# Batches 3 to 7 of a fused attention and feed-forward kernel: slots' maxima sent ahead of k and v, slots' work four units later in the plan, attention begun three units ahead

## The chip, the cores and the metric

One core of a Trainium2 chip runs the program. The metric is the device time in microseconds of one execution. The kernel before takes 735.24 us (median of three runs, 733.53 to 735.92).

## The reference, cut to what matters

Eight batches b, eight heads, 576 tokens, head width 64, and 32 memory slots per head. All in float32:

```
a    = softmax(phi, over the 32 slots' own token axis)      # as written: max, exp and sum over the 576 tokens
k_m  = a^T @ k ;  v_m = a^T @ v                             # 32 slots per head
attn = softmax(q @ k_m^T / 8, over the 32 slots)
x    = attn @ v_m, heads side by side                        # [4608, 512]
h    = x @ w_in                                             # [4608, 2048]
g    = where(h > 0, h, exp(min(h, 0)) - 1)
out  = g @ w_out                                            # [4608, 512]
```

phi's maximum over the tokens is one number for each head and slot, 256 numbers a batch, and exp(phi - max) is needed with tokens on the partitions, as the left side of a^T @ k.

## The kernel before, in words

**Attention of one batch.** phi comes twice: as `ph` (128 partitions of slots, 2 x 576 tokens, load_phi, L260) for the maxima and sums, and as three tiles `e` (tokens on the partitions, load_e, L267). phi_max (L407, DVE) takes the negative maxima `nm`, phi_exp (L412, ACT) the sums. spread_max (L272) brings the maxima to all partitions: one DMA writes `nm` (1 KB) to DRAM as `nmd` (L276), a second reads it back to 128 partitions as `nmb` (L278); it waits for the first. e_shift (L289, POOL, three instructions) adds `nmb` to `e`, e_exp (L294, ACT, three) takes the exponentials. slots (L453, PE, 80 small matmuls in one PSUM bank `psb`) makes k_m and v_m; slots_copy (L474, DVE), slots_transpose (L487, PE) and kv_copy (L494, ACT) turn them; scores (L502, PE), and a softmax in DVE and ACT for each of three token groups follow, ending in the tiles `A`. Then v_m is multiplied into w_in, in four pieces: vw (L502, PE) fills both `psb` banks, vw_high (L605, ACT) and vw_low (L611, DVE) split each bank into a high and a low part and give it back. There are two `psb` banks in all, taken in turn by vw, slots, slots_transpose and scores.

**Units.** The feed-forward part is a line of 256 units, 32 a batch, two token halves by 16 groups of 128 channels. Unit n is: hidden (L657, six matmuls into a bank `psh`, two of these), relu of -h (L672) and its exponential (L673) on ACT, elu_max on DVE (L684 for 256 tokens, L686 for the last 32, which also gives the `psh` bank back), elu_high (L698, ACT), elu_low (L704, DVE), project (L712, six matmuls into `pso`). After every second batch the 32 last tokens of the four halves are projected in one go: rest_high (L752), rest_low (L757), rest_project (L712), rest_store (L771 on ACT, then four DMAs, L773). store (L743) writes a half of a batch.

**What sets the order.** A table FIRST gives the order on all engines up to the start of batch 2's units. After it, `at(place, step, ...)` gives each step a place counted in units, and the steps are emitted by place: hidden of unit n at n - 1.7, project at n + 0.6, and attention of batch b from o = 32 b - 22 on. For PE and SP the order by place is the order on the engine. For ACT, DVE and POOL a scheduler chooses: it may put an instruction ahead of others with an earlier place. On each engine the instructions run in the order that results, and a wait holds all that stand behind it. SP runs ahead of the others as far as its waits let it: in each batch it stands at store until the last collect, and then issues the next batch's loads one after the other.

Of the kernel before, what the change touches and what calls it, by code (L numbers as in the profile page):

```python
# [8 lines left out]
F32 = mybir.dt.float32  # L9
# [7 lines left out]
P = 128  # L17
# [10 lines left out]
NB = 2  # L28
# [147 lines left out]
def fused_kernel(ctx: ExitStack, tc: tile.TileContext, phiT, phi, kv0, kvt, kv, q0, q1, w_in, w_out, out):  # L176
# [15 lines left out]
    dram = ctx.enter_context(tc.tile_pool(name="dram", bufs=2, space=bass.MemoryType.DRAM))  # L192
# [6 lines left out]
    def t2k(shape, name):  # L199
        return work.tile(shape, F32, name=name, tag="t2k", bufs=7)  # L200
# [11 lines left out]
    def temp(b, name, i, n):  # L212
# [20 lines left out]
    st = [  # L233
        {"kv": {}, "q": {}, "vw": [None] * NVC, "A": [None, None], "e": {}, "sc": {}, "ps": {}}
        for _ in range(B)
    ]
# [35 lines left out]
    def spread_max(b):  # L272

        s = st[b]
        d = dram.tile([P, 2], F32, name="nmd")
        nc.sync.dma_start(d, s["nm"])  # L276
        s["nmb"] = work.tile([P, P, 2], F32, name="nmb", bufs=1)
        nc.sync.dma_start(  # L278
            s["nmb"].rearrange("p x a -> p (x a)"),
            d.rearrange("x a -> (x a)").partition_broadcast(P),  # L280
        )
# [425 lines left out]
    acc = {}  # L707
# [61 lines left out]
    def rest_store(p):  # L769
        t = t2k([P, DM], "orest")  # L770
        nc.scalar.copy(t, acc.pop(("rest", p)))  # L771
        for n in range(4):
            nc.sync.dma_start(  # L773
                out[2 * p + n // 2, n % 2, NT * P :], t[n * REST : (n + 1) * REST, :]
            )
# [7 lines left out]
    def warm_up(n):  # L783
# [8 lines left out]
        for f in (  # L792
            tables, warm_up, load_phi, load_e, load_kv, load_kv0, load_q, load_half_q, load_raw, dec_mag,
            dec_low, dec_top, dec_add, dec_high, dec_rest, phi_max, phi_exp, slot_scale,
            spread_max, e_shift, e_exp, e_transpose, e_copy, slots, slots_copy, slots_transpose,
            kv_copy, scores, turn, softmax_max, softmax_shift, softmax_exp, softmax_sum,
            softmax_divide, turn_back, probs_high, probs_low, vw, vw_high, vw_low, hidden,
            elu_exp, elu_max, rest_copy, elu_high, elu_low, project, collect, store, rest_high, rest_low,
            rest_project, rest_store,
        )  # L800
    }
# [11 lines left out]
    def at(place, f, *a):  # L813
        if (f, a) not in done:
            plan.append((place, len(plan), f, a))

    def softmax(b, u, o, step):
        at(o, turn, b, u)
        at(o + step, softmax_max, b, u)
        at(o + 1.01 * step, softmax_shift, b, u)  # L820
        at(o + 2 * step, softmax_exp, b, u)
        at(o + 3 * step, softmax_sum, b, u)
        at(o + 3.01 * step, softmax_divide, b, u)
        at(o + 4 * step, turn_back, b, u)
        at(o + 5 * step, probs_high, b, u)
        at(o + 6 * step, probs_low, b, u)

    def products(b, c, o, *cols):
        at(o, vw, b, c, *cols)
        at(o + (0.3 if cols else 0.75), vw_high, b, c, *cols)  # L830
        at(o + (0.31 if cols else 0.76), vw_low, b, c, *cols)

    def attention(b, o):
        at(o - 4, load_phi, b)
        for c in range(NCH):
            at(o - 3 + c, load_kv, b, c)
        for u in range(3):
            at(o + 4 + u, load_q, b, u)
            at(o - 3 + u, load_e, b, u)
            at(o + 1.1 + u, e_shift, b, u)  # L840
            at(o + 2.1 + u, e_exp, b, u)
        at(o + 0.1, phi_max, b)
        for g in range(2):
            at(o + 0.12, phi_exp, b, g)
        at(o + 1.1, slot_scale, b)
        at(o + 1, spread_max, b)
        for c in range(NCH):
            at(o + 5.4, slots, b, c)
        at(o + 6.1, slots_copy, b)
        at(o + 7.2, slots_transpose, b)  # L850
        at(o + 7.4, kv_copy, b)
        for u in range(3):
            i = o + 8.2 + 2 * u
            at(i, scores, b, u)
            softmax(b, u, i + 0.7, 0.3)

    for b in range(2, B):
        base = 2 * NJ * b
        attention(b, 43 if b == 2 else base - 22)
        for c in range(NVC):  # L860
            products(b, c, base - 7.6 + 8 * c)
    for it, (b, hf, j) in enumerate(order):
        at(it - 1.7, hidden, it)
        at(it - 1.69, elu_exp, it)
        at(it - 1.68, elu_max, it)
        if b < NB:
            at(it - 1.67, rest_copy, it)
        at(it - 1, elu_high, it)
        at(it - 0.99, elu_low, it)
        at(it + 0.6, project, it)  # L870
        if ends[it][2]:
            for t in range(NT):
                at(it + 0.7, collect, it, t)
            if j == NJ - 1:
                at(it + 0.8, store, b, hf)
                if b % 2 and hf:
                    for i in range(NJ // 2):
                        at(it + 0.61 + 0.01 * i, rest_high, b // 2, i)
                        at(it + 0.611 + 0.01 * i, rest_low, b // 2, i)
                        at(it + 0.612 + 0.01 * i, rest_project, b // 2, i)  # L880
                    at(it + 0.81, rest_store, b // 2)

    plan.sort(key=lambda x: x[:2])
    with tc.manual_schedule(engines={mybir.EngineType.PE, mybir.EngineType.SP}):
# [48 lines left out]
```

## Time and profile before

| what | value |
|---|---|
| median of three runs | 735.24 us |
| the profiled execution's own time | 735.4 us |
| its span, first to last instruction | 733.6 us |
| mean granted TensorE clock | 0.99 |
| PE busy | 709.2 us, 97% |
| DVE, ACT, POOL busy | 467.2, 465.0, 44.6 us |

A row of the timeline has the start in us, the duration, the engine, the line, the operation with out<-in, the count of instructions that it merges, and in brackets how long the engine stood idle before it and what ended that. SPq is SP's queue of DMA issues. A row of the waits names the engine and line that waited, what it waited for, and then the total in us, the number of times and the longest. A row of the stretches has the two ends in us, then the length, the busy time of each engine, the granted TensorE clock, the DMA share and GB/s.

### The profile page before, as it was taken

What the parts mean: (1) busy time and instruction counts of PE and PEld (TensorE: products, weight loads), DVE (VectorE), ACT (ScalarE), POOL (GpSimd) and SP (SyncE); (2) the same over time, 40 slices, a digit from 0 to 9 for tenths busy, and PEclk for the clock granted to TensorE, in tenths of its full rate; (3) what the DMA queues carried; (4) which work ended last, traced back from release to release, by engine and by line L of the source; (5) the groups of instructions that cost most, each with busy time, mean ns of one, the idle gap of its engine ahead of it and who ended that gap; (6) DMA issues with size and microseconds to landing.
All of it is one profiled execution on the core that took longest, in us unless ns stands there. A gap on an engine that the chain in (4) does not pass through costs nothing.

```text
span 733.6 us, 13668 instructions
## 1 busy us (share of the span) xinstructions
PE 709.2 (97%) x5114; PEld 572.5 (78%) x5114; DVE 467.2 (64%) x1253; ACT 465.0 (63%) x1110; POOL 44.6 (6%) x88
## 2 busy tenths in 40 slices
PE   7688999999999999999999999999999999999997
PEld 6566888888768878877788777887787887888885
DVE  4999899886495467544954449545774447754442
ACT  4768988886456656755655557656565565665552
POOL 0001112123000100010000100000000010000000
PEclk9899999999999999999999999999999999999999
DMA  8960513431316110611015210260002600010002
GB/s 311 370 231 28 203 30 115 149 101 62 101 59 210 28 44 1 239 42 45 2 57 182 56 45 1 75 206 28 18 1 75 218 27 20 1 58 0 2 1 72
DMA packets 24978, 64.46 MB, mean 88 GB/s; under 512 B 3408, under 2 KB 7632, under 8 KB 24912
## 3 DMA queue, kind: packets, MB, share of 16 engines
q1 hardware_dynamic: 24912, 63.59, 25.7%
q8 instruction: 41, 0.67, 0.4%
q14 instruction: 25, 0.20, 0.1%
HBM read 54.13 MB, written 9.44 MB: 87 GB/s over the span
## 4 chain that ended last, share of the span: by engine, by line
PE 68%; DMA 14%; DVE 8%; ACT 5%; issue 2%; POOL 1%; SPq 1%; POOLq 0%; DVEq 0%; ACTq 0%
PE pso L712 41%; PE psh L657 21%; DMA nmd<-nm 6%; PE psb L502 4%; DMA nmb<-nmd 3%; PE psb L453 2%; DMA ph<-phiT 2%; POOL e L289 1%; DMA win<-w_in 1%; ACT gf L673 1%; DMA kvt<-kv 1%; ACT gf L672 1%; DMA e<-phi 1%; DVE gf L681 1%; DVE nm L407 1%
## 5 line engine op out<-in xcount | busy, mean ns | idle before, releaser
L712 PE MATMUL pso<-wout,gp 128*128 128x512 f32 x1728 | 449.6, 398 | 3.3 <-DVE gp L704 2.6
L712 PEld LDWEIGHTS pso<-wout,gp 128*128 128x128 f32 x1728 | 310.1, 188 | 84.2 <-ACT gf L673 13.0
L657 PEld LDWEIGHTS psh<-A,vw 128*128 128x128 f32 x1536 | 229.9, 189 | 39.5 <-issue 6.2
L657 PE MATMUL psh<-A,vw 128*128 128x288 f32 x1536 | 251.1, 299 | 8.6 <-DVE rest L686 3.8
L684 DVE SCALAR_TENSOR_TENSOR gf<-gf,psh 128x256 f32<-128x256 f32 x192 | 80.4, 419 | 130.3 <-ACT gf L673 130.0
L672 ACT ACTIVATE gf<-psh 128x288 f32<-128x288 f32 x256 | 104.7, 409 | 86.3 <-PE psh L657 84.4
L698 ACT CAST gp<-gf 128x256 fp32r<-128x256 f32 x256 | 103.4, 404 | 87.0 <-DVE gf L684 73.4
L704 DVE TENSOR_TENSOR gp<-gf,gp 128x256 fp32r<-128x256 f32 x256 | 107.6, 421 | 55.0 <-ACT gp L698 54.7
L673 ACT ACTIVATE gf<-gf 128x288 f32<-128x288 f32 x256 | 113.7, 444 | 7.8
L611 DVE TENSOR_TENSOR vw<-psb,vw 128x512 fp32r<-128x512 f32 (+2 forms) x74 | 43.3, 602 | 11.7 <-ACT vw L605 11.5
L289 POOL TENSOR_TENSOR e<-e,nmb 128x512 f32<-128x512 f32 (+1 forms) x18 | 19.7, 1122 | 377.1 <-DMA nmb<-nmd 374.8
L681 DVE SCALAR_TENSOR_TENSOR gf<-gf,psh 128x288 f32<-128x288 f32 x64 | 28.9, 452 | 18.2 <-ACT gf L673 16.9
L605 ACT CAST vw<-psb 128x512 fp32r<-128x512 f32 (+2 forms) x74 | 37.1, 522 | 2.9 <-PE psb L502 0.7
L502 PE MATMUL psb<-win,kvm 64*32 64x512 f32 (+2 forms) x592 | 36.0, 541 | 0.0
L694 POOL COPY rest<-gf 128x32 f32<-128x32 f32 x64 | 24.3, 380 | 167.6 <-DVE gf L681 167.5
L686 DVE SCALAR_TENSOR_TENSOR rest<-gf,psh 128x32 f32<-128x32 f32 x192 | 34.2, 179 | 0.1
L752 ACT CAST gp<-rest 128x256 fp32r<-128x256 f32 x32 | 13.0, 406 | 23.8 <-PE pso L712 21.8
L373 DVE SCALAR_TENSOR_TENSOR top<-mag,top 128x512 uint32<-128x512 uint32 x32 | 22.2, 692 | 1.9 <-ACT mag L364 0.3
L757 DVE TENSOR_TENSOR gp<-rest,gp 128x256 fp32r<-128x256 f32 x32 | 13.4, 418 | 15.0 <-ACT gp L752 14.9
L368 ACT ACTIVATE mag<-raw 128x512 uint32<-128x512 uint32 x30 | 20.0, 670 | 2.5 <-DVE top L373 2.5
L294 ACT ACTIVATE e<-e 128x512 f32<-128x512 f32 (+1 forms) x18 | 9.8, 559 | 16.9 <-POOL e L289 16.8
L364 ACT ACTIVATE mag<-raw 128x512 f32<-128x512 f32 x30 | 19.5, 668 | 0.4 <-DVE win L385 0.4
(96 smaller groups left out, 368.4 us busy)
## 6 DMA issues: line engine op xcount, KB each, us to landing
kvt<-kv SPq DMA_DIRECT2D x32, 512.0 KB, 7.4
out<-osb SPq DMA_DIRECT2D x16, 512.0 KB, 2.8
raw<-w_in SPq DMA_DIRECT2D x15, 512.0 KB, 6.0
raw<-w_out SPq DMA_DIRECT2D x15, 512.0 KB, 7.9
qt<-q SPq DMA_DIRECT2D x18, 384.0 KB, 4.3
ph<-phiT SPq DMA_DIRECT2D x7, 576.0 KB, 5.0
e<-phi SPq DMA_DIRECT2D x12, 256.0 KB, 6.3
qh<-q SPq DMA_DIRECT2D x4, 576.0 KB, 11.5
```

Of the source, the lines that this page charges most:

```text
L502: nc.tensor.matmul(outs[a][32 * j : 32 * j + 32, :], lhs[r, 32 * j : 32 * j + 32], rhs[r, j], start=True, stop=True, tile_position=(64 * a ...
L605: nc.scalar.copy(s["vw"][c][:, HI, a, n0:n1], ps)
L611: nc.vector.tensor_tensor(t[:, LO, a, n0:n1], ps, t[:, HI, a, n0:n1], ALU.subtract)
L657: nc.tensor.matmul(ps, t[:, x, g, c0 : c0 + P], s["A"][hf][:, y, g, :], start=(n == 0), stop=(n == 5),)
L672: nc.scalar.activation(gf, ps, AF.Relu, scale=-1.0)
L673: nc.scalar.activation(gf, gf, AF.Exp, scale=-1.0)
L681: nc.vector.scalar_tensor_tensor(gf, gf, -1.0, ps, ALU.add, ALU.max)
L684: nc.vector.scalar_tensor_tensor(gf[:, :n], gf[:, :n], -1.0, ps[:, :n], ALU.add, ALU.max)
L686: nc.vector.scalar_tensor_tensor(rest_of(b, j)[:, o : o + REST], gf[:, n:], -1.0, ps[:, n:], ALU.add, ALU.max)
L698: nc.scalar.copy(gp[:, HI], gs[it][:, : NT * P])
L704: eng.tensor_tensor(gp[:, LO], gf[:, : NT * P], gp[:, HI], ALU.subtract)
L712: nc.tensor.matmul(ps, gp[:, y], wout[j][:, x, :], start=(first and n == 0), stop=(last and n == 2),)
```

## The change: what it does

In attention(b) for b of 3 to 7 (x = 1; batch 2 keeps its places):

- o is 32 b - 25, three units earlier, and with it load_phi and load_e; phi_max, phi_exp and the DMA that writes `nmd` go one more unit ahead.
- spread_max only writes `nmd`; the reading DMA is a step of its own, fetch_max, at o + 1.5. load_kv's five loads begin at o + 1, so that the write of `nmd` stands ahead of all of them, and fetch_max behind the first.
- e_shift, e_exp, slots, slots_copy, slots_transpose, kv_copy and scores get four units (4.4 for the first two) on top of o, so that slots to scores lie one unit later than before in the line of units. load_q lies two units later.
- rest_store keeps the copy on ACT; its four DMAs become rest_out, at the unit's place + 4.6 in place of + 0.81.

```diff
     def spread_max(b):
 
         s = st[b]
-        d = dram.tile([P, 2], F32, name="nmd")
+        d = s["nmd"] = dram.tile([P, 2], F32, name="nmd")
         nc.sync.dma_start(d, s["nm"])
+        if b <= NB:
+            fetch_max(b)
+
+    def fetch_max(b):
+        s = st[b]
+        d = s["nmd"]
         s["nmb"] = work.tile([P, P, 2], F32, name="nmb", bufs=1)
...
     def rest_store(p):
         t = t2k([P, DM], "orest")
         nc.scalar.copy(t, acc.pop(("rest", p)))
+        acc["orest", p] = t
+
+    def rest_out(p):
+        t = acc.pop(("orest", p))
         for n in range(4):
...
     def attention(b, o):
+
+        x = 1 if b > NB else 0
         at(o - 4, load_phi, b)
         for c in range(NCH):
-            at(o - 3 + c, load_kv, b, c)
+            at(o - 3 + 4 * x + c, load_kv, b, c)
         for u in range(3):
-            at(o + 4 + u, load_q, b, u)
+            at(o + 4 + 5 * x + u, load_q, b, u)
             at(o - 3 + u, load_e, b, u)
-            at(o + 1.1 + u, e_shift, b, u)
-            at(o + 2.1 + u, e_exp, b, u)
-        at(o + 0.1, phi_max, b)
+            at(o + 1.1 + 4.4 * x + (1 - 0.3 * x) * u, e_shift, b, u)
+            at(o + 2.1 + 4.4 * x + (1 - 0.3 * x) * u, e_exp, b, u)
+        at(o + 0.1 - x, phi_max, b)
...
-        at(o + 1, spread_max, b)
+        at(o + 1 - x, spread_max, b)
+        if b > NB:
+            at(o + 1.5, fetch_max, b)
         for c in range(NCH):
-            at(o + 5.4, slots, b, c)
-        at(o + 6.1, slots_copy, b)
...
+            at(o + 5.4 + 4 * x, slots, b, c)
+        at(o + 6.1 + 4 * x, slots_copy, b)
...
         for u in range(3):
-            i = o + 8.2 + 2 * u
+            i = o + 8.2 + 4 * x + 2 * u
...
-        attention(b, 43 if b == 2 else base - 22)
+        attention(b, 43 if b == 2 else base - 25)
...
                     at(it + 0.81, rest_store, b // 2)
+                    at(it + 4.6, rest_out, b // 2)
```

The changed file has new lines, so that what is L294 before is L300 in it, and so on: 6 more from L278 on.

**ACT, batch 4's e_exp.** Before, the relu that reads psh_3890 is that of unit 105, and e_exp (L294) stands behind it:

```order
L672 ACTIVATE gf_3897<-psh_3890 128x288
L673 ACTIVATE gf_3897<-gf_3897 128x288
L698 CAST gp_3912<-gf_3897 128x256
L294 ACTIVATE e_3885<-e_3885 128x512
L672 ACTIVATE gf_3922<-psh_3915 128x288
L294 ACTIVATE e_3910<-e_3910 128x512
L673 ACTIVATE gf_3922<-gf_3922 128x288
L605 CAST vw_3950<-psb_3927 128x512
L294 ACTIVATE e_3945<-e_3945 64x256
```

After, the relu that reads psh_3825 is that of unit 102, and e_exp is L300:

```order
L704 CAST gp_3822<-gf_3809 128x256
L678 ACTIVATE gf_3832<-psh_3825 128x288
L679 ACTIVATE gf_3832<-gf_3832 128x288
L300 ACTIVATE e_3820<-e_3820 128x512
L704 CAST gp_3845<-gf_3832 128x256
L300 ACTIVATE e_3843<-e_3843 128x512
L678 ACTIVATE gf_3855<-psh_3848 128x288
L300 ACTIVATE e_3866<-e_3866 64x256
L679 ACTIVATE gf_3855<-gf_3855 128x288
```

The plan's place of e_exp is later than before, but on ACT it stands three units earlier, ahead of the elu_high of unit 102 (L704 that writes gp_3845); in batches 3, 5, 6 and 7 it stands 4, 4.5, 3.5 and 4.5 units earlier.

**PE, batch 4's slots.** Before, slots (L453) follows a hidden, and vw (L502) comes a project and a hidden behind it:

```order
L657 MATMUL psh_4107<-A_3476,vw_3950 128x288 x6
L453 MATMUL psb_4119<-kvt_3883,e_3885 32x128 x8
L453 MATMUL psb_4119<-kvt_3908,e_3885 32x128 x8
L453 MATMUL psb_4119<-kvt_3943,e_3910 32x128 x8
L453 MATMUL psb_4119<-kvt_3973,e_3910 32x128 x8
L453 MATMUL psb_4119<-kvt_4001,e_3945 32x128 x8
L712 MATMUL pso10_3768<-wout7_1317,gp_4080 128x512 x3
L712 MATMUL pso11_3769<-wout7_1317,gp_4080 128x512 x3
L657 MATMUL psh_4173<-A_3405,vw_3950 128x288 x6
L502 MATMUL psb_4185<-win3_80,kvm_3305 32x512 x4
L502 MATMUL psb_4186<-win3_80,kvm_3305 32x512 x4
```

After (vw is L508, slots L459), the two have the same place, and slots stands right behind vw:

```order
L663 MATMUL psh_4126<-A_3426,vw_3960 128x288 x6
L508 MATMUL psb_4138<-win3_80,kvm_3326 32x512 x4
L508 MATMUL psb_4139<-win3_80,kvm_3326 32x512 x4
L459 MATMUL psb_4148<-kvt_3917,e_3820 32x128 x8
L459 MATMUL psb_4148<-kvt_3955,e_3820 32x128 x8
L459 MATMUL psb_4148<-kvt_3983,e_3843 32x128 x8
L459 MATMUL psb_4148<-kvt_4006,e_3843 32x128 x8
L459 MATMUL psb_4148<-kvt_4029,e_3866 32x128 x8
L718 MATMUL pso00_3740<-wout8_1591,gp_4100 128x512 x3
```

With two banks, slots' psb_4148 is the bank that vw's psb_4138 has just filled, and its first matmul waits for DVE. The order is the same in all five batches.

**SP, batch 7's loads**, behind the stores of batch 5 (the loads of batch 5, behind the stores of batch 3, read the same). Before:

```order
L773 DMA out<-orest 32x512 x4
L260 DMA ph<-phiT 128x1152
L300 DMA kvt<-kv 128x1024
L267 DMA e<-phi 128x2x256
L300 DMA kvt<-kv 128x1024
L267 DMA e<-phi 128x2x256
L300 DMA kvt<-kv 128x1024
L267 DMA e<-phi 64x256
L300 DMA kvt<-kv 128x1024
L300 DMA kvt<-kv 64x1024
L276 DMA nmd<-nm 128x2
L278 DMA nmb<-nmd 128x256
```

After:

```order
L260 DMA ph<-phiT 128x1152
L783 DMA out<-orest 32x512 x4
L267 DMA e<-phi 128x2x256 x2
L267 DMA e<-phi 64x256
L276 DMA nmd<-nm 128x2
L306 DMA kvt<-kv 128x1024
L284 DMA nmb<-nmd 128x256
L306 DMA kvt<-kv 128x1024 x3
L306 DMA kvt<-kv 64x1024
L328 DMA qt<-q 128x768 x3
```

The maxima (L276) have moved ahead of all five loads of k and v, phi's load ahead of the rest's stores, and the loads of `e` still stand behind those stores. In batches 4 and 6 there is no rest in front. On DVE, batch 3's phi_max has moved from behind unit 68 into the end of FIRST, between batch 2's turn_back (L567) and its last rest_low instructions (L757); that of batches 5 and 7 into the rest stage; that of batches 4 and 6 stands where it stood.

More of the change, by code (lines that the diff above doesn't have):

```diff
@@ L833, in attention @@
     def attention(b, o):
+        x = 1 if b > NB else 0
         at(o - 4, load_phi, b)
         for c in range(NCH):
-            at(o - 3 + c, load_kv, b, c)
+            at(o - 3 + 4 * x + c, load_kv, b, c)
         for u in range(3):
-            at(o + 4 + u, load_q, b, u)
+            at(o + 4 + 5 * x + u, load_q, b, u)
             at(o - 3 + u, load_e, b, u)
-            at(o + 1.1 + u, e_shift, b, u)
-            at(o + 2.1 + u, e_exp, b, u)
-        at(o + 0.1, phi_max, b)
+            at(o + 1.1 + 4.4 * x + (1 - 0.3 * x) * u, e_shift, b, u)
+            at(o + 2.1 + 4.4 * x + (1 - 0.3 * x) * u, e_exp, b, u)
+        at(o + 0.1 - x, phi_max, b)
         for g in range(2):
-            at(o + 0.12, phi_exp, b, g)
+            at(o + 0.12 - x, phi_exp, b, g)
         at(o + 1.1, slot_scale, b)
-        at(o + 1, spread_max, b)
+        at(o + 1 - x, spread_max, b)
+        if b > NB:
+            at(o + 1.5, fetch_max, b)
         for c in range(NCH):
-            at(o + 5.4, slots, b, c)
-        at(o + 6.1, slots_copy, b)
-        at(o + 7.2, slots_transpose, b)
-        at(o + 7.4, kv_copy, b)
+            at(o + 5.4 + 4 * x, slots, b, c)
+        at(o + 6.1 + 4 * x, slots_copy, b)
+        at(o + 7.2 + 4 * x, slots_transpose, b)
+        at(o + 7.4 + 4 * x, kv_copy, b)
         for u in range(3):
-            i = o + 8.2 + 2 * u
+            i = o + 8.2 + 4 * x + 2 * u
             at(i, scores, b, u)
```

## The prediction

> **What bounds the kernel now.** First the page's busy times, then the waits of PE and ACT from batch 3's loads to the end:
>
> ```profile
> PE 709.2 (97%) x5114; PEld 572.5 (78%) x5114; DVE 467.2 (64%) x1253; ACT 465.0 (63%) x1110; POOL 44.6 (6%) x88
> PE psh L657 <- DVE rest L686: 3.8, 5, 1.1
> PE pso L712 <- DVE gp L704: 0.3, 1, 0.3
> ACT e L294 <- POOL e L289: 14.6, 8, 3.3
> ```
>
> PE bounds the kernel. From batch 3 on it waits 4.1 us in all (3.8 + 0.3), once in each of the five batches. Each time ACT stands at e_exp for POOL's e_shift, and POOL for the maxima. Batch 4's chain, from the timeline:
>
> ```profile
> 305.33 1.35 DVE L407 TENSOR_REDUCE nm<-ph 128x2 f32<-128x1152 f32 x1 [0.52 <-DMA ph<-phiT]
> 307.23 0.33 SPq L276 DMA_DIRECT2D nmd<-nm  x1
> 315.32 0.33 SPq L278 DMA_DIRECT2D nmb<-nmd  x1
> 320.13 3.29 POOL L289 TENSOR_TENSOR e<-e,nmb 128x512 f32<-128x512 f32 x3 [76.53 <-DMA nmb<-nmd]
> 321.48 0.63 ACT L294 ACTIVATE e<-e 128x512 f32<-128x512 f32 x1 [3.19 <-POOL e L289]
> 324.09 0.18 DVE L686 SCALAR_TENSOR_TENSOR rest<-gf,psh 128x32 f32<-128x32 f32 x1
> 324.41 1.04 PE L657 MATMUL psh<-A,vw 128*128 128x288 f32 x6 [0.96 <-DVE rest L686]
> ```
>
> The write of 1 KB takes 8.1 us (307.23 to 315.32), behind k and v in the queue; from the read's issue to e_exp it is another 6.16 us. ACT stands 3.19 us, PE loses 0.96 of it.
>
> **Term 1: e_exp's wait, removed.** If it went altogether: **-4.1 us**.
>
> **Term 2: e_exp's wait, come back longer.** The maxima are now ahead of k and v. The nearest row for a write with nothing in front is batch 2's:
>
> ```profile
> 169.32 0.34 SPq L276 DMA_DIRECT2D nmd<-nm  x1
> 172.48 0.33 SPq L278 DMA_DIRECT2D nmb<-nmd  x1
> ```
>
> 3.16 us. With the 6.16 from above, e_exp's data are there 9.32 us after the write is issued: call that time T. In batch 4 phi_max stands where it stood, so the write goes out at about 307.0, and T = 316.3: 5.2 us sooner than 321.48. But on ACT e_exp stands three units sooner, behind unit 102's exponential:
>
> ```profile
> 310.66 0.44 ACT L673 ACTIVATE gf<-gf 128x288 f32<-128x288 f32 x1
> 314.12 1.55 PE L712 MATMUL pso<-wout,gp 128*128 128x512 f32 x6
> 315.51 0.96 PE L657 MATMUL psh<-A,vw 128*128 128x288 f32 x6
> ```
>
> ACT comes to it at 311.1 and stands 5.2 us. Queued behind it are unit 102's elu_high, which project 102 (314.12) waits for, and unit 103's relu, whose bank hidden 105 (315.51) needs. By the old chain's steps (two e_exp at 0.54, POOL 1.3 apart, relu, exponential, L684, L686) elu_low ends 1.4 us after T and the bank is free 3.6 after T. So project 102 starts at 317.7 (3.6 late), hidden 105 at 319.9: **4.4 us** lost. Batch 6 has the same order, and the same 4.4.
>
> In batches 5, 7 and 3 the loads of `e` stand behind the rest's stores, and the write behind those. Batch 5, and batch 3's rows:
>
> ```profile
> 391.99 1.74 SPq L773 DMA_DIRECT2D out<-orest  x4
> 394.75 0.43 SPq L267 DMA_DIRECT2D e<-phi  x1
> 395.28 0.41 SPq L300 DMA_DIRECT2D kvt<-kv  x1
> 405.53 0.96 PE L657 MATMUL psh<-A,vw 128*128 128x288 f32 x6
> 219.25 1.76 SPq L773 DMA_DIRECT2D out<-orest  x4
> 234.57 0.96 PE L657 MATMUL psh<-A,vw 128*128 128x288 f32 x6
> ```
>
> An issue takes 0.53 us (394.75 to 395.28), so three `e` end at 393.75 + 1.6, the write goes at 395.4, and T = 404.7. Here e_exp stands behind elu_high, as before, and the bank is free 2.93 us after T (324.41 - 321.48): hidden 136 starts at 407.6 instead of 405.53, **2.1**. Batch 7 is laid out alike, 2.1. Batch 3: write at 222.7, T = 232.0, two e_exp ahead of elu_high and the third ahead of the next relu, bank 4.1 after T: 236.1 instead of 234.57, **1.5**. Sum: 4.4 + 4.4 + 2.1 + 2.1 + 1.5 = **+14.5 us**. Bounds: the shortest landing of a store in the profile is 1.7 us, of a load 3.0:
>
> ```profile
> out<-orest SPq DMA_DIRECT2D x16, 64.0 KB, 1.7
> ph<-phiT SPq DMA_DIRECT2D x2, 288.0 KB, 3.0
> kvt<-kv SPq DMA_DIRECT2D x32, 512.0 KB, 7.4
> ```
>
> With these T comes 1.5 + 1.5 us sooner (1.7 for 3.16, and 3.0 for the read's 4.5 or so): 1.4 lost in batches 4 and 6, nothing in the others, +2.8. On the other side the first load of k and v lies between write and read and three 512 KB loads right behind: 1 us more a batch, +19.5. I keep 14.5, since batch 2 is the same transfer.
>
> **Term 3: slots wait for vw's bank, added.** slots now stands on PE right behind vw, and wants the bank that vw_low gives back. Before, slots_transpose wanted the same bank a project later, in batch 4:
>
> ```profile
> 341.32 1.09 PE L502 MATMUL psb<-win,kvm 64*32 64x512 f32 x16
> 342.34 1.65 PE L712 MATMUL pso<-wout,gp 128*128 128x512 f32 x6
> 343.07 0.69 DVE L611 TENSOR_TENSOR vw<-psb,vw 128x512 fp32r<-128x512 f32 x1 [0.21 <-ACT vw L605]
> 343.83 0.42 PE L487 MATMUL psb<-ident,x 128*128 128x128 f32 x2
> ```
>
> The next matmul behind vw starts 1.02 us after it (342.34); the bank is usable 2.51 after it (343.83). The whole line of projects and hiddens stands behind slots. 1.49 us in each of five batches: **+7.5 us**. Lower bound 0.3 a batch, what slots_transpose itself lost there:
>
> ```profile
> PEld psb L487 <- DVE vw L611: 1.3, 5, 0.3
> ```
>
> **Term 4: batch 3's phi_max, moved.** It goes from a DVE that had time into the end of FIRST, where PE waits for DVE's rest_low:
>
> ```profile
> 214.51 0.42 DVE L757 TENSOR_TENSOR gp<-rest,gp 128x256 fp32r<-128x256 f32 x1
> 214.98 1.43 PE L712 MATMUL pso<-wout,gp 128*128 128x512 f32 x5 [0.57 <-DVE gp L757]
> 225.99 1.34 DVE L407 TENSOR_REDUCE nm<-ph 128x2 f32<-128x1152 f32 x1
> ```
>
> PE already waits, so all 1.34 us count: **+1.3** (0 if phi's reduction fits a gap).
>
> **Term 5: the clock.** PE's pauses grow from 1 us to over 3. What pauses do to the granted clock is seen near the start, in stretches of 3.41 us:
>
> ```profile
> 19.77:23.18 3.41, 1.49 (x25) 1.15 (x24) 3.20 (x8) 2.47 (x7) 0.00 (x0) 0.99 1.03 408
> 23.18:26.60 3.42, 3.01 (x44) 2.46 (x46) 3.32 (x8) 2.76 (x6) 0.00 (x0) 0.51 1.03 409
> 36.84:40.25 3.41, 1.89 (x21) 1.37 (x10) 3.31 (x8) 2.50 (x5) 0.00 (x0) 0.99 1.02 408
> 40.25:43.66 3.41, 3.41 (x24) 2.00 (x23) 3.38 (x10) 2.06 (x7) 0.21 (x1) 0.51 1.02 408
> 57.30:60.73 3.43, 2.17 (x22) 1.26 (x21) 3.36 (x11) 3.43 (x9) 0.00 (x0) 1.00 0.00 0
> 60.73:64.10 3.37, 2.32 (x16) 1.86 (x14) 3.30 (x12) 2.01 (x6) 0.34 (x1) 1.00 0.00 0
> ```
>
> A stretch with PE idle for 1.92 (3.41 - 1.49) or 1.52 us is followed by one at 0.51; one with 1.26 idle is not. At 0.51 a stretch loses at most 3.41 x 0.49 = 1.67 us. The pauses of batches 4 to 7 (3.6, 2.1, 3.6, 2.1) are beyond the edge; those of batch 3 and of slots (1.5) lie on it. Four drops at 1.3, since part of a slow stretch is pause: **+5.2** (0 to 12 drops: 0 to 15).
>
> The Trainium skill ("TensorE: Matmul & The Clock Gate", Why this matters for your kernels) asks for no PE gap over some 3 us; by that only batches 4 and 6 would lose clock, and the term would be 2.6. The trace disagrees: 1.52 us was enough.
>
> **At nothing.** k and v land 7.4 us after issue and are needed only at slots, some 20 us later; if late, slots waits. load_q keeps its distance to scores. rest_out changes only SP: the last batch's four stores stay last. phi_max and phi_exp of batches 5 and 7 fall into rest-stage pauses of DVE and ACT; uncovered, under 1.3 each. vw's first piece comes one unit closer behind the last scores; uncovered, some 0.5 a batch.
>
> **Sum:** -4.1 + 14.5 + 7.5 + 1.3 + 5.2 = +24.4, on the profiled execution's 735.4 (0.2 above the median): **760 us**.
>
> **The rivals.**
>
> - *Clock by the longer edge.* Only pauses over 3 us cost clock: two drops, 757 us. For it: all other stretches of the kernel run at 1.00. Against: the 1.52 row. 0.13. (It is the rule of the Trainium skill's page "TensorE: Matmul & The Clock Gate", named under term 5.)
> - *Clock at every pause.* Batch 3's and slots' pauses, six more drops at 1.3, +7.8: 768. They lie between the rows of 1.26 and 1.52, and need to fall into one stretch. 0.15.
> - *The maxima come soon.* Landings at the profile's shortest: term 2 is 2.8, no pause exceeds 1.5, term 5 is 0: 735.4 - 4.1 + 2.8 + 7.5 + 1.3 = 743. Against: batch 2's 3.16 with an empty queue. 0.14. The Trainium skill ("DMA: Bandwidth & Descriptors", Anatomy of one DMA) gives a fixed 2 us for a transfer; two and POOL's 1.3 would make T the write's issue + 5.3, and then no e_exp would hold PE in batches 3, 5 and 7; by it the sum would be some 741 us.
> - *Faster: the head start is enough.* e_exp finds its data, PE's 4.1 us go, and the bank costs its lower bound, 0.26 a batch: 735.4 - 4.1 + 1.3 + 1.3 = 734, or 732.6 if phi_max fits a gap. It decides in ACT at 311.1: T must come within 5 us of the write. Against: two dependent transfers, the order on PE. 0.03.
>
> **How the numbers follow.** My forecast has 0.52; 0.03 is left for no change. 0.3% (2.2 us) is about what a measurement of this kernel can tell from no change. All but the last two cases are slower: 0.94. The range takes in both clock rivals: its low end, 745, is term 2 at 5 us with no drop of the clock (735.4 - 4.1 + 5 + 7.5 + 1.3), its high end, 771, the clock at every pause (768) with 3 of the 5 us that term 2's upper bound adds. The 743 us rival lies just outside it.
>
> **What would show it.** ACT's wait for POOL's e grows to some 4 to 5 us in batches 4 and 6; PE waits at L718 and L663 behind it; PE waits some 1.5 us for DVE L617 at slots (L459) five times; the write lands in about 3 us; stretches of 0.5 clock follow pauses. It is wrong if ACT's wait shrinks, if slots starts without a wait, or if the clock stays at 1.00.

## The result, and the profile after

The changed kernel takes 773.2 us (median of 6 runs, 768.7 to 774.0), the kernel before 735.4 in the same comparison (6 runs, 733.5 to 736.6): ratio 1.050, 95% interval 1.048 to 1.052. It is slower, as forecast; the forecast of 760 was 13 us short, and the upper end of its range, 771, 2 us short. The profiled execution of after is its fastest: 768.7 us, span 766.9, which is 33.3 more than before's span of 733.6.

The page's busy times, and then the waits of the whole engines from 200 us on (us in total, times, longest):

```profile
PE 717.5 (94%) x5114; PEld 579.8 (76%) x5114; DVE 467.2 (61%) x1253; ACT 466.6 (61%) x1110; POOL 44.6 (6%) x88
```

```profile
ACT e L300 <- POOL e L295: 30.2, 10, 6.4
PE pso L718 <- ACT gp L704: 11.0, 3, 4.0
PE psh L663 <- DVE rest L692: 9.6, 3, 4.9
PE psb L459 <- issue: 7.3, 5, 1.5
PE pso L718 <- DVE gp L763: 1.9, 1, 1.9
```

ACT's wait at e_exp has doubled, from 14.6 us to 30.2. PE stands behind it for 11.0 + 9.6 = 20.6 us, where it was 4.1. Slots (L459) waits five times, 1.46 us each; the view names "issue" and not vw_low, but the five places are those right behind vw. And the wait at the end of FIRST (L763) has grown from 0.57 to 1.88 us. PE's busy time has grown by 8.3 us with the same 5114 matmuls: most of that is a lower clock.

Batch 5 shows the whole chain; its rows from the timeline (start, duration, then the engine):

```profile
403.15 1.75 SPq L783 DMA_DIRECT2D out<-orest  x4
404.95 1.48 SPq L267 DMA_DIRECT2D e<-phi  x3
406.53 0.53 SPq L276 DMA_DIRECT2D nmd<-nm  x1
407.16 0.38 SPq L306 DMA_DIRECT2D kvt<-kv  x1
411.49 0.33 SPq L284 DMA_DIRECT2D nmb<-nmd  x1
411.91 0.38 SPq L306 DMA_DIRECT2D kvt<-kv  x1
```

```profile
415.30 1.55 PE L718 MATMUL pso<-wout,gp 128*128 128x512 f32 x6
417.15 3.21 POOL L295 TENSOR_TENSOR e<-e,nmb 128x512 f32<-128x512 f32 x3 [93.30 <-DMA nmb<-nmd]
418.46 0.63 ACT L300 ACTIVATE e<-e 128x512 f32<-128x512 f32 x1 [5.55 <-POOL e L295]
421.04 0.18 DVE L692 SCALAR_TENSOR_TENSOR rest<-gf,psh 128x32 f32<-128x32 f32 x1
421.36 1.06 PE L663 MATMUL psh<-A,vw 128*128 128x288 f32 x3 [4.51 <-DVE rest L692]
```

From the write's issue to the read's issue it is 4.96 us (406.53 to 411.49), not 3.16. From the read's issue to e_exp it is 6.97 (411.49 to 418.46), not 6.16. So T is 11.9 us and not 9.32. The bank is free 2.9 us after e_exp (421.36), as forecast; all of the error is in T. In batch 7 something is added. Its three loads of e take longer to issue than batch 5's (2.87 us against 1.48), so the write goes out 1.4 us later:

```profile
592.62 2.87 SPq L267 DMA_DIRECT2D e<-phi  x3
```

Over batches 3 to 7 the write takes 4.9, 3.7, 5.0, 4.6 and 4.1 us in this trace, and T is 11.8, 10.2, 11.9, 11.0 and 10.9.

Batch 4, where ACT comes to e_exp before elu_high:

```profile
311.55 0.34 SPq L276 DMA_DIRECT2D nmd<-nm  x1
315.27 0.33 SPq L284 DMA_DIRECT2D nmb<-nmd  x1
```

```profile
321.76 0.63 ACT L300 ACTIVATE e<-e 128x512 f32<-128x512 f32 x1 [5.80 <-POOL e L295]
322.29 0.39 ACT L704 CAST gp<-gf 128x256 fp32r<-128x256 f32 x1
322.73 2.42 PE L718 MATMUL pso<-wout,gp 128*128 128x512 f32 x6 [3.69 <-ACT gp L704]
325.33 1.78 PE L663 MATMUL psh<-A,vw 128*128 128x288 f32 x6 [0.18 <-DVE rest L692]
```

Here the loss is 3.69 + 0.18 = 3.9 us against a forecast of 4.4. T is 0.9 longer than forecast, but elu_high stands behind the first e_exp and not behind the second, so the project starts 1.0 us after T and not 1.4. It also runs longer, 2.42 us and not 1.55. So the hidden behind it, which starts 3.6 us after T as forecast, hardly has to wait: part of its delay is counted as busy time.

What the pause does to the clock is seen in stretches of 3.41 us laid on the clock's own steps (columns as before: PE busy first, the granted clock after POOL's). Batch 7:

```profile
604.00:607.41 3.41, 0.53 (x3) 0.09 (x1) 0.00 (x0) 0.89 (x2) 2.20 (x2) 1.00 1.02 405
607.41:610.82 3.41, 1.41 (x6) 1.44 (x7) 1.34 (x5) 2.46 (x7) 1.00 (x2) 0.50 1.00 217
610.82:614.24 3.42, 3.42 (x11) 2.86 (x11) 1.50 (x6) 1.60 (x4) 0.00 (x0) 0.50 0.07 23
614.24:617.65 3.41, 3.41 (x32) 2.45 (x31) 0.94 (x3) 1.84 (x5) 0.00 (x0) 1.00 0.00 0
```

The pause fills most of the first stretch and reaches into the second, and both are followed by one at 0.50: in the second slow stretch PE does 11 matmuls, in the next, at 1.00, 32. In this execution there are seven such stretches behind the pauses of batches 4 to 7 (one, two, two, two), none behind batch 3's.

One more cost is seen in the row of vw's first piece behind the last scores:

```profile
285.47 1.46 PE L508 MATMUL psb<-win,kvm 64*32 64x512 f32 x16
285.86 0.15 PEld L508 LDWEIGHTS psb<-win,kvm 64*32 64x32 f32 x8 [0.24 <-DVE sc L531]
```

vw takes 1.46 us instead of 1.09, since its second half waits for the bank that DVE's turn (L531) empties. Scores has come one unit closer to it. This is 0.37 us, five times, 1.8 us.

### The profile page after: what moved, and what is told of

It reads as the page before. It is cut to its first block, busy times and chain, and to the rows that moved or that the text cites. A ratio compares the mean times of both kernels' runs of the same rounds, so it can differ in the third digit from the quotient of the medians.

```text
span 766.9 us, 13662 instructions
## 1 busy us (share of the span) xinstructions
PE 717.5 (94%) x5114; PEld 579.8 (76%) x5114; DVE 467.2 (61%) x1253; ACT 466.6 (61%) x1110; POOL 44.6 (6%) x88
## 4 chain that ended last, share of the span: by engine, by line
PE 74%; DMA 9%; DVE 8%; ACT 4%; issue 3%; POOL 1%; SPq 0%; POOLq 0%; DVEq 0%; ACTq 0%
PE pso L718 44%; PE psh L663 23%; PE psb L508 5%; DMA nmb<-nmd 3%; DMA nmd<-nm 3%; PE psb L459 2%; DMA ph<-phiT 1%; DMA win<-w_in 1%; ACT gf L679 1%; POOL e L295 1%; DVE gf L687 1%; DMA e<-phi 1%; ACT gf L678 1%; DVE top L379 1%; DVE vw L617 1%
## 5 line engine op out<-in xcount | busy, mean ns | idle before, releaser
L718 PE MATMUL pso<-wout,gp 128*128 128x512 f32 x1728 | 453.1, 400 | 15.5 <-ACT gp L704 11.2
L663 PEld LDWEIGHTS psh<-A,vw 128*128 128x128 f32 x1536 | 233.1, 191 | 43.4 <-ACT e L300 10.2
L704 ACT CAST gp<-gf 128x256 fp32r<-128x256 f32 x256 | 103.6, 405 | 85.7 <-DVE gf L690 73.9
L508 PE MATMUL psb<-win,kvm 64*32 64x512 f32 (+2 forms) x592 | 37.6, 538 | 0.3 <-DVE win L391 0.3
L300 ACT ACTIVATE e<-e 128x512 f32<-128x512 f32 (+1 forms) x18 | 10.0, 556 | 32.8 <-POOL e L295 32.8
L379 DVE SCALAR_TENSOR_TENSOR top<-mag,top 128x512 uint32<-128x512 uint32 x32 | 22.2, 692 | 1.9 <-ACT mag L370 0.3
L459 PEld LDWEIGHTS psb<-kvt,e 128*32 128x32 f32 (+1 forms) x480 | 12.3, 109 | 13.9 <-issue 13.9
L459 PE MATMUL psb<-kvt,e 128*32 128x128 f32 (+1 forms) x480 | 15.8, 275 | 7.3 <-issue 7.3
```

The source lines that it names most:

```text
L459: nc.tensor.matmul(ps[32 * j : 32 * j + 32, a], s["e"][c // 2][:r, c % 2, x : x + M], kv_rows(b, c, i, 2 * j + a), start=(c == 0 and a == ...
L508: nc.tensor.matmul(outs[a][32 * j : 32 * j + 32, :], lhs[r, 32 * j : 32 * j + 32], rhs[r, j], start=True, stop=True, tile_position=(64 * a ...
L663: nc.tensor.matmul(ps, t[:, x, g, c0 : c0 + P], s["A"][hf][:, y, g, :], start=(n == 0), stop=(n == 5),)
L704: nc.scalar.copy(gp[:, HI], gs[it][:, : NT * P])
L718: nc.tensor.matmul(ps, gp[:, y], wout[j][:, x, :], start=(first and n == 0), stop=(last and n == 2),)
```

## Experiments

All ratios are to the kernel before, run beside the experiment on the same chip. Experiments 1 to 3 and the first of 8 ran on one chip (before: 731.4 us), all others on a second one (before: 732.4 and 732.3); both run before 3 to 4 us faster than the first comparison's chip. The changed kernel was run again on the second one only (experiment 9): ratio 1.054 there, 1.050 in the first comparison. Edits are shown against the changed kernel unless said otherwise.

**1. slots one unit sooner** (the rest of the order unchanged).

```diff
-            at(o + 5.4 + 4 * x, slots, b, c)
+            at(o + 5.4 + 3 * x, slots, b, c)
```

> Only slots of batches 3 to 7 goes one unit sooner in the order, off its place behind vw. Theory (slots waits for vw's bank, five times 1.46 us in the changed kernel's trace): those 7.3 us go, slots_transpose waits 0.3 us instead as before (1.3 in all): 773.2 - 7.3 + 1.3 = 767 us, 765 if the bank costs nothing any more; PE shows no wait at slots, and e_exp's waits stay (20 to 23 us). Rival (the bank is wanted by somebody anyway, so that the wait only moves to slots_transpose or scores): 772 to 774.

Measured: 763.5 us against 731.4, ratio 1.043 (1.039 to 1.047), where the changed kernel has 1.050. PE's waits from 200 us on:

```profile
PE pso L718 <- ACT gp L704: 9.4, 3, 3.5
PE psh L663 <- DVE rest L692: 8.7, 2, 4.8
PE pso L718 <- DVE gp L763: 1.9, 1, 1.9
```

The row of slots is gone and no other has come for it; e_exp's waits stay (18.1 us). 0.7% of 735 are 5.4 us, which agrees with the expected 6; the changed kernel did not run on this chip, and against its 1.054 on the other one it would be 8. The rival, that the wait only moves, is out. Term 3 stands.

**2. e_exp held.** e_exp's plan place is moved, and in the stretch of the plan that holds it ACT follows the plan (elsewhere the scheduler orders it). It comes to stand some six units later.

```diff
-            at(o + 1.1 + 4.4 * x + (1 - 0.3 * x) * u, e_shift, b, u)
-            at(o + 2.1 + 4.4 * x + (1 - 0.3 * x) * u, e_exp, b, u)
+            at(o + 1.1 + 1.0 * x + (1 - 0.9 * x) * u, e_shift, b, u)
+            at(o + 2.1 + 1.9 * x + (1 - 0.3 * x) * u, e_exp, b, u)
...
-        for _, _, f, a in plan:
-            f(*a)
+        for inside, part in itertools.groupby(plan, lambda x: held(x[0])):
+            with tc.manual_schedule(engines=act) if inside else contextlib.nullcontext():
+                for _, _, f, a in part:
+                    f(*a)
```

Here `act` is PE, SP and ACT, and `held` is true from 22.2 to 18.5 units ahead of a batch's base.

> Only e_exp's place on ACT changes: in batches 3 to 7 it is held to some six units later than in the changed kernel, behind elu_high of units 76 to 79 (batch 3), so that its data are there. Maxima, loads and slots stay as changed. Theory (ACT stands at e_exp, and PE behind it): PE's 21.5 us of waits behind ACT go, and the clock's loss with them (6 to 11 us): 773.2 - 21.5 - 6 to 11 = 741 to 746 us, clock 1.00 from batch 3 on. Rival 1 (the clock's loss has another cause, such as the slots' pauses): about 752. Rival 2 (the maxima or the five loads in another order cost by themselves, through contention; or slots now waits for e_exp): over 755.

Measured: 739.0 us against 731.4, ratio 1.011 (1.008 to 1.014): 3.9% of the 5.0% are gone by this edit alone, 29 us. PE's waits:

```profile
PE psb L459 <- issue: 7.3, 5, 1.5
PE pso L718 <- DVE gp L763: 1.9, 1, 1.9
```

ACT's and PE's waits for e_exp are gone, and the clock stays at 1.00 from 40 us on until PE's work is done. On 735.4 the ratio gives 743.6, inside the theory's 741 to 746. Rival 1, that the clock falls for another reason, is out, and so is rival 2. (In the stretch that is held, the rest of ACT follows the plan too; what that does by itself was not tried.)

**3. Both edits together.**

> slots one unit sooner and e_exp held, together; the maxima still go ahead of k and v. Theory (the early maxima are good, and the loss is all in the two places): before's 735.4 less its five waits for e_exp (4.1), plus batch 3's phi_max at the end of FIRST (1.3): 732.6 us, 731 to 734. Rival (the early loads and maxima cost something of their own): 736 or more.

Measured: 734.1 us against 731.4, ratio 1.003 (1.001 to 1.005). My expectation was wrong by 0.7%: it put this kernel 2.8 us under before, and it is 2.7 over. In its trace PE waits only at L763 (1.9 us), so what before loses at e_exp is not lost here. Two things were missing in the sum. One is vw's first piece, which is as slow here as in the changed kernel:

```profile
282.61 1.45 PE L508 MATMUL psb<-win,kvm 64*32 64x512 f32 x16
283.00 0.15 PEld L508 LDWEIGHTS psb<-win,kvm 64*32 64x32 f32 x8 [0.23 <-DVE sc L531]
```

The other may lie in before itself, which this chip runs 4 us faster: it may lose less at e_exp here than in the first trace.

**4. before again**, profiled on the second of the faster chips.

> The kernel before, unchanged, profiled on the chip of these runs (its runs on the chip of the first four experiments had a median of 731.4 us, where the profiled execution shown first had 735.4). If the missing gain of slots sooner and e_exp held (734.1 against 731.4) is a matter of the chip, PE's waits at L657 for DVE, 3.8 us in the first trace, are shorter here, under 1.5 us. Rival (the early loads cost something of their own): they are 3.8 us here too.

Measured: 730.1 us, and in its trace:

```profile
PE psh L657 <- DVE rest L686: 1.2, 2, 0.8
PE pso L712 <- DVE gp L757: 0.6, 1, 0.6
ACT e L294 <- POOL e L289: 10.7, 8, 3.1
```

PE loses 1.2 us at e_exp and not 4.1. From the write's issue to e_exp it takes 13.6 us on average over batches 3 to 7, in the first trace 14.3: 0.7 us of a transfer's time decide over most of that wait. So in this execution term 1 is worth 1.2 us. It is one execution, 2.3 us under the median of before on its chip (732.4), and whether the chip or the execution makes the difference is not shown. With 1.2, experiment 3 adds up: -1.2 + 1.3 (phi_max) + 1.8 (vw) + up to 1.7 for the slow stretch that its trace has behind the wait at L763 (as in experiment 10) gives 1.9 to 3.6, and 2.7 was measured. Experiment 3 ran on another chip than this trace, so this sum is argued and not shown.

**5. before's order, with the maxima early.** The two edits, and slots' copies, transposes and scores also one unit sooner, so that TensorE's order is before's; batch 3's phi is loaded, and its phi_max and phi_exp done, six units sooner, where DVE has time.

```diff
+        y = 6 if b == NB + 1 else 0
-        at(o - 4, load_phi, b)
+        at(o - 4 - y, load_phi, b)
-        at(o + 0.1 - x, phi_max, b)
+        at(o + 0.1 - x - y, phi_max, b)
...
-            i = o + 8.2 + 4 * x + 2 * u
+            i = o + 8.2 + 3 * x + 2 * u
```

> e_exp held, and slots, its copies and scores all back at before's places on PE (TensorE's order is before's); only the maxima and their write stay ahead of k and v; batch 3's phi is loaded, and its phi_max done, six units sooner, off the end of FIRST. Theory (all the loss lies in the places; the early maxima take away before's waits for e_exp): before less its waits for e_exp, of 4.1 us where they are as in the first trace, and less what the last scores cost by standing one unit closer to vw (0.36 us each in the trace of the kernel with both edits): 0 to 4 us under before, ratio 0.994 to 1.000. Rival (the early loads cost something of their own, as both edits' +0.3% would have it): ratio 1.002 or more.

Measured: 729.1 us against 732.4 (9 and 13 runs), ratio 0.9961 (0.9947 to 0.9975). PE's waits, and vw's first piece:

```profile
PE pso L718 <- DVE gp L763: 0.6, 1, 0.6
```

```profile
279.47 1.09 PE L508 MATMUL psb<-win,kvm 64*32 64x512 f32 x16
```

This kernel is faster than both. The maxima ahead of k and v are good; e_exp finds its data and PE does not wait. The rival (the early loads cost something of their own) is out. The gain of 3.4 us lies between the two values that the traces have for term 1, 1.2 and 4.1 us. The trace of before on this chip has only 1.2 of it; that the executions nearer the median wait longer would fit, but no trace shows it.

**6. The write ahead of the loads of e.** In batches 4 and 6 the scheduler also puts e_exp one unit later on ACT.

```diff
-            at(o - 3 + u, load_e, b, u)
+            at(o - 3 + 3.05 * x + (1 - 0.99 * x) * u, load_e, b, u)
```

> The changed kernel with the write of the maxima ahead of the three loads of e in the queue; in batches 4 and 6 e_exp comes one unit later on ACT. Theory (the write lands late since it shares the queue with the loads in front of it): the write takes 3 us instead of 3.7 to 5.0, and from its issue to e_exp it is 9.5 us instead of 10.2 to 11.9; PE's waits behind e_exp fall by some 1.5 us a batch: 7 to 9 us less, and 2 or 3 drops of the clock of 1.5 us fewer: 763 us on the chip of the first runs. Rival (the delay is not the queue's, or passes on to the read, which now stands behind the loads): T stays at 11, the time within 2 us of the changed kernel's, apart from the one unit in batches 4 and 6 (4 us).

Measured: 756.2 us against 732.4, ratio 1.033 (1.031 to 1.036; the changed kernel 1.054 on this chip, experiment 9). Batch 5:

```profile
406.25 0.37 SPq L276 DMA_DIRECT2D nmd<-nm  x1
406.66 1.49 SPq L267 DMA_DIRECT2D e<-phi  x3
410.10 0.34 SPq L284 DMA_DIRECT2D nmb<-nmd  x1
```

```profile
417.45 0.63 ACT L300 ACTIVATE e<-e 128x512 f32<-128x512 f32 x1 [3.30 <-POOL e L295]
```

Against experiment 9's trace, on the same chip, the write is hardly faster, 3.8 us on average against 4.0, and the read, now behind the loads, is slower: 7.6 us to e_exp against 6.7. T is 11.4 and not 10.7. So the part of the theory that is about T falls, and the rival is right there: the delay is passed on. The time fell all the same, by 14 us (756.2 against 770.2) and not only by the 4 us of the one unit: in batches 3, 5 and 7 the write goes out 1.5 to 2.7 us sooner before the matmuls that PE then waits for, since it no longer stands behind the issues of three loads (1.49 us in batch 5). ACT waits 3.30 us there and not 4.83, and PE stands 12.0 us behind e_exp in all and not 18.7. The rest fits the clock, though no trace divides it: its mean in these runs is 0.976 to 0.984, in experiment 9's 0.969 to 0.973 but for one.

**7. The read ahead of the first load of k and v.**

```diff
-            at(o + 1.5, fetch_max, b)
+            at(o + 0.9, fetch_max, b)
```

> The changed kernel with the read of the maxima ahead of the first load of k and v (SyncE then waits for the write with nothing issued behind it). Theory (the 512 KB of k and v in front of the read delay it): from the read's issue to e_exp it is 6.2 us, as in the kernel before, instead of 6.4 to 7.0; 0.6 us a batch: 3 us less. If the first load also delays the write, the write takes 3.2 us and it is 8 us less. Rival (the loads behind the read, issued at once, delay it all the same): 0 to 1 us less.

Measured: 766.4 us against 732.4, ratio 1.047 (1.0446 to 1.0495). Batch 4 here, and in experiment 9's trace of the changed kernel, on the same chip:

```profile
313.47 0.35 SPq L276 DMA_DIRECT2D nmd<-nm  x1
316.41 0.34 SPq L284 DMA_DIRECT2D nmb<-nmd  x1
316.80 3.67 SPq L306 DMA_DIRECT2D kvt<-kv  x5
```

```profile
311.50 0.34 SPq L276 DMA_DIRECT2D nmd<-nm  x1
311.88 0.43 SPq L306 DMA_DIRECT2D kvt<-kv  x1
315.02 0.33 SPq L284 DMA_DIRECT2D nmb<-nmd  x1
```

With no load issued behind it the write takes 2.94 us here and not 3.52, and in each of the five batches 0.56 to 0.89 us less, 3.4 on average and not 4.0. The read gains nothing, 7.0 us to e_exp against 6.7; five loads now follow it at once. T is 10.3, 0.4 less. So the one 512 KB load issued right behind the write made it 0.6 us slower; batch 2's write, from which I took 3.16 us, has nothing behind it. What is left over 2.94 is in batches 3, 5 and 7 (3.7, 3.9 and 3.2), where stores and the loads of e are just ahead; that these are the reason is not shown. PE stands 15.7 us behind e_exp and not 18.7, and the time is 3.8 us under the changed kernel's on this chip, with the intervals apart (1.052 to 1.057 there). That is more than the rival's 0 to 1 us, and less than the 8 us of the theory's second case, since the read got slower.

**8. The pauses filled**, twice: 9 to 13 matmuls of the identity at each of the five places where PE waits behind e_exp.

```diff
+    def keep(n):
+        ps = bank([P, P], "b")
+        for _ in range(n):
+            nc.tensor.matmul(ps, ident, ident, start=True, stop=True)
...
+    for place, n in ((70.59, 9), (102.59, 10), (134.29, 12), (166.59, 11), (198.29, 13)):
+        plan.append((place, len(plan), keep, (n,)))
```

> The changed kernel, with 9 to 13 matmuls of the identity into an unused bank put on PE at each of the five places where it waits behind e_exp (2.8 to 4.0 us of work in pauses of 3.3 to 4.9 us); nothing else is moved, so the waits' ends stay. It computes the same output. Theory (PE's idle time in a stretch of 3.41 us lowers the clock of the next one): no stretch at 0.5 behind these places, 6 to 11 us less: 762 to 767 us. Rival (the clock's loss is not caused by the pauses, or costs nothing since what it slows would wait anyway): 772 to 774; if the added matmuls end later than the waits: up to 776.

Measured: 761.9 us against 731.4, ratio 1.041 (1.037 to 1.044). The clock has no stretch at 0.50 behind the pauses. To see the difference on one chip it was repeated beside the changed kernel:

> The changed kernel with 9 to 13 matmuls of the identity in each of the five pauses, once more, now beside the changed kernel on one chip. Theory (what the pauses cost through the clock is the fifth term, and 5.5 to 7 us in all): 5 to 9 us under the changed kernel. Rival (the 7 us between the first runs were the chip's): within 2 us of it.

Measured: 763.3 us (4 runs, 761.0 to 764.6), the changed kernel 770.2 beside it: 6.9 us. With ratios 1.043 (1.040 to 1.045) and 1.054 (1.052 to 1.057) the intervals are apart. PE has more to do, e_exp comes no sooner, and the kernel is 6.9 us faster: that is what the pauses cost through the clock.

**9. The changed kernel again**, on the chip of the last one.

> The changed kernel, unchanged, on the same chip as the kernel with its pauses filled. Ratio to before 1.048 to 1.054, as in its first runs; PE's waits behind e_exp 20 to 23 us, seven stretches of the clock at 0.5, give or take two, behind the five pauses.

Measured: median 770.2 us, ratio 1.054 (1.052 to 1.057). One execution, the profiled one, took 763.2 at a mean clock of 0.987, the other four 768.8 to 772.7 at 0.969 to 0.973. Its waits behind e_exp are 18.7 us, 1.9 less than in the first profile of this kernel, which does not explain 6 to 9 us. But it has three slow stretches behind the pauses and not seven. Batch 4's pause there, and batch 5's:

```profile
317.62:321.03 3.41, 1.65 (x10) 1.29 (x8) 0.00 (x0) 0.00 (x0) 0.82 (x1) 1.00 0.96 245
321.03:324.45 3.42, 1.88 (x6) 1.05 (x6) 0.56 (x2) 2.56 (x6) 2.58 (x3) 1.00 1.04 349
324.45:327.86 3.41, 2.81 (x17) 2.54 (x17) 1.93 (x7) 2.32 (x6) 0.00 (x0) 1.00 0.40 101
416.60:420.01 3.41, 0.60 (x4) 0.63 (x5) 0.89 (x3) 2.89 (x8) 1.80 (x2) 1.00 1.05 202
420.01:423.42 3.41, 3.41 (x12) 2.84 (x11) 1.94 (x7) 1.95 (x5) 0.00 (x0) 0.50 0.22 66
```

Batch 4's pause of over 3 us falls half into one stretch (idle 1.76) and half into the next (1.54), and neither is followed by a slow one. Batch 5's falls into one (idle 2.81), and it is. So the same waits cost more or less by where the stretches happen to begin. My expectations of seven, give or take two, and of 20 to 23 us of waits, missed that. Of the other four executions only the time and the mean clock are known.

**10. phi_max back at the end of FIRST** (experiment 5 with `y = 0`).

> As the kernel with before's order and the maxima early, but batch 3's phi_max again at the end of FIRST, as in the changed kernel. Theory (PE's wait for L763 grows from 0.6 to 1.9 us, and the pause is followed by a stretch of 3.41 us at 0.5 in part of the executions): 1.3 to 3 us more than that kernel, a ratio to before of 0.998 to 1.000. Rival (the wait is made up later): 0.996, as that kernel.

Measured: 731.7 us against 732.3 (12 and 16 runs), ratio 0.9997 (0.998 to 1.001), 0.4% or 2.7 us over experiment 5. The wait, and the stretch behind it:

```profile
PE pso L718 <- DVE gp L763: 1.9, 1, 1.9
```

```profile
214.45:217.87 3.42, 1.55 (x7) 1.05 (x6) 3.35 (x11) 1.76 (x5) 0.00 (x0) 1.00 0.00 0
217.87:221.28 3.41, 3.41 (x12) 3.01 (x11) 2.85 (x8) 1.36 (x3) 0.00 (x0) 0.50 0.00 0
```

The 1.3 us of term 4 are there, and about as much again through the clock: 1.88 us of waiting in one stretch can be enough (in experiment 2's trace the same wait was not followed by a slow stretch). The theory stands; the rival (made up later) is out.

## Why the prediction was right in sign and short in size

By its terms, in the profiled execution of after (differences to before's profiled execution):

| term | forecast | measured | from |
|---|---|---|---|
| 1. old waits at e_exp | -4.1 | -4.1 | none of them is left as it was |
| 2. new waits at e_exp | +14.5 | +20.6 | 11.0 + 9.6 |
| 3. slots behind vw | +7.5 | +7.3 | the row of L459 |
| 4. phi_max in FIRST | +1.3 | +1.3 | 1.88 - 0.57 |
| 5. clock | +5.2 | +6.5 | PE busy 8.3 more, less 1.8 for vw |
| vw behind the last scores | 0 | +1.8 | 5 x 0.37 |
| sum | +24.4 | +33.4 | spans differ by 33.3 |

The other five executions had a lower mean clock (0.965 to 0.972 against 0.976) and took 770.0 to 774.0; the last 4.4 us up to the median fit the lower clock and experiment 9's mechanism, but no trace of those executions shows them.

- **Term 1** is right in the trace it was read from. It is not the same in every execution: 1.2 us in experiment 4's.
- **Term 2 is the step that failed**, in "I keep 14.5, since batch 2 is the same transfer". It isn't: behind batch 2's write nothing is issued, behind these a load of 512 KB. T was 11.2 us on average and not 9.32: the write took 4.5 and not 3.16, the read 6.7 to e_exp and not 6.16. Experiment 7 shows about half of what the write took too long: without that load it takes 0.6 us less (batch 4: 2.94 us; in the nine traces with the load 3.35 to 3.72). For the other half, and for the read, the cause stays open; in batches 3, 5 and 7 the rest's stores and three loads of e are just ahead as well. By batch (3 to 7) PE lost 3.3, 3.9, 4.5, 4.0 and 4.9 us; forecast were 1.5, 4.4, 2.1, 4.4 and 2.1. That PE stands behind e_exp is right in all five, and so are the places on ACT; in batch 3 it stands at the project, for elu_high, and not at the bank as forecast. In batches 4 and 6 T was too short too, by 0.9 and 1.7 us, and the losses are near by luck: the project that waits runs longer (2.42 and 3.06 us, not 1.55), and so part of the delay counts as busy time. In the three odd batches T was taken 1.6 to 2.6 us too short, and "Batch 7 is laid out alike" missed the 1.4 us by which its write goes out later. I had set the price of the neighbours, 1 us a batch, only into the upper bound (19.5). The measured 20.6 lies over that too.
- **Term 3** is right, to 0.03 us a batch, and experiment 1 shows that it is a loss of its own.
- **Term 4** is right as a wait; its own slow stretch, some 1.4 us in experiment 10, was in no term; in the profile of after it did not come.
- **Term 5** is right in kind and a little small: 6.5 in the profile, 6.9 in experiment 8, more in the median. That it is so near is in part luck. Its edge, between 1.26 and 1.52 us of idle time, was too low for this part of the kernel. The count of drops was too low, seven and not four, since a pause of 4 us can give two. The price of 1.3 us each was too high: from 205 us on PE is busy 9.2 us longer, or 7.4 without vw, some 1.05 for each of the seven. (The first 205 us, where nothing was changed, came out 0.9 shorter.)
- **"At nothing"** was wrong for vw's first piece, which I had priced at 0.5 a batch if uncovered and then left out: 0.37, five times. For the rest of that paragraph (k and v, q, rest_out, phi_max of batches 5 and 7) no wait shows in the trace.
- **The rivals.** "The maxima come soon" and "the head start is enough" needed T at some 6 us or e_exp later; T was 10 to 12. (The 1.7 and 3.0 us that the first goes by are medians of a group of transfers, and not the shortest landings.) The rule of the Trainium skill ("DMA: Bandwidth & Descriptors", Anatomy of one DMA) of a fixed 2 us for a transfer, which that section gives for transfers issued from GpSimd, is less than the fastest write in any trace here, 2.66 us (batch 2's, in experiment 4), issued from SyncE. "Clock by the longer edge" falls by experiment 10's row, 1.88 us of waiting followed by a stretch at 0.50, and by the 19 of 19 cases below; so does the rule behind it. "Clock at every pause" falls too: slots' five pauses of 1.46 us never lowered it, nor did batch 3's of 3.3 us, which in the profile of after was cut in two (idle 1.73 and 1.61).
- **The signs** named ahead: ACT's wait in batches 4 and 6 was 5.8 and 6.4 us where 4 to 5 was forecast; slots waits five times; slow stretches follow pauses; the write landed in 3.7 to 5.0 us and not in 3.

## What to carry to other kernels

Sending a dependent transfer sooner is not enough where a scheduler then puts its consumer sooner too, on an engine that runs in order (why it did so here is not shown). Look where the consumer has moved to, and hold it back behind work that does not need the data (experiment 2 gave back 29 of 38 us). Take a small transfer's time from a row with the same neighbours in its queue, behind it as well as ahead. And price a pause of TensorE twice, once as a wait and once through the clock, which added about a third here (6.5 us on 20.6 in the first trace).

## What the runs showed of the hardware

- The clock goes by stretches of 3.41 us: in each of the 13 traces all its changes lie on one grid of that length, from the first to the last, whatever the pauses. Over the traces of before, of after and of the eleven experimental runs, after their first 200 us and from stretches at 1.00: idle time of PE of 1.88 us or more was followed by a stretch at 0.50 in 19 of 19 cases, of 1.30 to 1.45 us in 0 of 25, between 1.46 and 1.87 in 7 of 19. That is about half of a stretch. So a pause of 3.3 us can cost the clock nothing, when it is cut in two (experiment 9), and one of 1.88 us can cost 1.4 (experiment 10). The Trainium skill ("TensorE: Matmul & The Clock Gate", Why this matters for your kernels) has some 3 us of gap as the edge; here 1.88 in one stretch was enough in every case.
- A write of 1 KB took 2.9 to 3.9 us with nothing issued behind it, and 3.5 to 4.5 with a load of 512 KB issued right after it (one trace each, on one chip, experiments 7 and 9; less in each of the five batches, 0.6 on average). A load behind a transfer delays it, not only one ahead.
- The chips differ by 0.4 to 0.6% in the median time of before (735.4, 732.4 and 731.4 us). In two traces of it, from two chips, 0.7 us less for its two dependent transfers goes with PE's wait at e_exp falling from 4.1 us to 1.2.
